# A planner that keeps VectorE and GpSimd apart at a shared port, with its priorities set anew, in a fused attention and two-expert-layer kernel

## The chip, the cores and the metric

The kernel runs on one core of a Trainium2 chip: TensorE (PE) with its weight loads (PEld), VectorE (DVE), ScalarE (ACT), GpSimd (POOL) and the queue engine SyncE (SP). The metric is the device time of one execution in microseconds. Before the change the median of three runs was 1277.99 us (1277.92 to 1278.14).

## The reference

Three steps follow each other on 2304 tokens of 512 numbers. The weights of the dense layer come as 64-bit floats; all else is fp32.

```python
# attention: 4 batches, 8 heads, 576 rows of 64; only the 32 largest scores of a row stay
scores = scale * np.matmul(q, k.transpose(0, 1, 3, 2))
kth = np.partition(scores, -32, axis=-1)[..., -32:-31]
scores = np.where(scores >= kth, scores, -1e9)
attn = softmax(scores);  x = attn @ v            # then heads side by side: (2304, 512)
# dense layer, 512 -> 2048 -> 512
h = x @ w_in;  x = (h * np.cos(h)) @ w_out
# 8 experts, 512 -> 1024 -> 512, one for each token
logits = x @ w_gate;  e_idx = np.argmax(logits, axis=1)
out[mask] = gate_w[mask, None] * eom[mask, e, None] * (np.maximum(x[mask] @ w1[e], 0) @ w2[e])
```

## The kernel before

The program is written as a list of operations (`plan.op`), each with its engine, an assumed length in ns, the buffers that it reads and writes, and a priority number. `Plan.run` plays this list through once while the program is being built, with the assumed lengths: whenever an engine is free it takes, among the operations that can start within 1 ns, the one with the lowest priority number, or else the one that can start first. What comes out is one fixed order for each engine. On the chip each engine works its order off in sequence and waits at semaphores for data and buffers; the assumed times themselves are not in the program. An operation held up on an engine therefore holds up all that stands behind it there.

Attention is cut into 80 units: 64 of two heads by 128 rows ("m") and 16 of two heads by the 64 rows that are left ("x"). In a unit (`attention`) PE transposes the queries (L555) and multiplies with the keys (L573); ACT copies the upper half of the scores (L581); DVE takes maxima and minima of the halves (L587) and finds the 32 largest by MAX8 and MATCH_REPLACE8 (L600, L605, L610); POOL prepares the threshold (L614), ACT and POOL mask the scores (L624, L628), ACT takes the exponential (L631), PE transposes (L652) and multiplies with the values (L683, L686), DVE normalises (L696), ACT and POOL split the result into two parts of less precision (L710, L712). Unit u has priority 10 u, plus an offset for each step from the table `ADD`. `load_heads` (L495 to L522) loads a pair of heads, `LOAD_AHEAD` before its first unit.

Beside it the 64-bit weights of the dense layer are converted in 32 pieces (`narrow`, L721 to L737): a load of 512 KB, two TENSOR_SCALAR on DVE (L722, L724), three ACT operations, an addition and a multiplication on POOL (L733, L735), and a SCALAR_TENSOR_TENSOR on DVE (L737). 16 pieces stay on the core (L745, L747), 16 are split (L755, L757) and stored to memory as `wod`. `CONV_RATE` says how many pieces there are for each unit.

The dense layer works on nine chunks of 256 tokens, eight units each (`moe_unit`, `moe_tail`): 24 matmuls into the hidden layer (L773 to L775), a cosine on ACT (L789), a product on DVE (L812), a split on ACT and POOL (L823, L825), a load of `wod` (L820) and 12 matmuls back (L833 to L835). `MOE_STEP` is the distance in priority from one unit of a chunk to the next. After each chunk `route` finds every token's expert with some 25 small DVE operations (L883 to L925), and POOL scatters the tokens' numbers into a table in memory (L929). The last scatter, reading the table back (L998) and gathering the tokens (L1037) lie between the dense layer and the experts.

The experts' weights are loaded in eight pieces each (L1014), copied by ACT in reduced precision (L1015), and what the copy loses is subtracted out by POOL (L1018) and DVE (L1022) in turn. `turn` transposes an expert's tokens on PE (L1053), with a copy on ACT (L1058) and a subtraction on DVE (L1060); `TURN_AT` sets its place among the matmuls of the expert before (L1077 to L1079, L1095 to L1097).

## Time and profile before

| | |
|---|---|
| median of three runs | 1277.99 us |
| profiled execution | 1275.37 us |
| its span, first to last instruction | 1273.6 us |
| PE busy | 1126.0 us, 88% |
| DVE busy | 881.9 us, 69% |
| ACT busy | 850.7 us, 67% |
| POOL busy | 717.9 us, 56% |

The profile is of one execution. A busy share over the whole span mixes stages: weight conversion beside the first attention units, attention beside the dense layer, and the experts alone. So the rows below are taken by stretches. "Idle before" of an instruction says what its engine waited for.

### The profile page before, as it was taken

How to read it: one execution, taken by the hardware profiler on the slowest of the kernel's cores; microseconds unless marked ns; L12 is line 12 of the kernel's file. 1: busy time of each engine (PE TensorE's matmuls, PEld its weight loads, DVE VectorE, ACT ScalarE, POOL GpSimd, SP SyncE). 2: the span in 40 equal slices, each digit the busy share in tenths (PEclk: the TensorE clock that was granted, in tenths of full speed). 3: DMA queues.
4: the chain of work that ended last, by engine and by line, in shares of the span. 5: the costliest groups of instructions: out<-in, count | busy, mean ns of one | idle time of the engine just before them, and what ended most of it. 6: DMA issues, size and time to landing. Idle time of an engine off the chain costs nothing.

```text
span 1273.6 us, 22562 instructions
## 1 busy us (share of the span) xinstructions
PE 1126.0 (88%) x7524; PEld 931.1 (73%) x7525; DVE 881.9 (69%) x2732; ACT 850.7 (67%) x1852; POOL 717.9 (56%) x1102
## 2 busy tenths in 40 slices
PE   3667778799999999899998989999973999999995
PEld 2444666578787787786776777878962899999994
DVE  6999989896899797979845899886233344443310
ACT  5888797877788887887766688888553344444320
POOL 7898879876546646544643546545447355554400
PEclk9777899989999999999999999999995999999998
DMA  7433325555604444225244403325686244344100
GB/s 196 131 132 126 98 67 173 187 167 186 212 17 130 117 147 133 67 84 166 95 130 130 150 2 109 100 75 164 207 307 212 87 168 158 132 150 156 62 19 25
DMA packets 95806, 164.71 MB, mean 129 GB/s; under 512 B 49850, under 2 KB 54202, under 8 KB 95680
## 3 DMA queue, kind: packets, MB, share of 16 engines
q1 hardware_dynamic: 91264, 153.71, 37.7%
q0 software_dynamic: 4416, 9.47, 2.3%
q8 instruction: 61, 1.00, 0.3%
q14 instruction: 65, 0.53, 0.1%
HBM read 146.72 MB, written 19.56 MB: 131 GB/s over the span
## 4 chain that ended last, share of the span: by engine, by line
PE 43%; DVE 23%; ACT 13%; issue 9%; POOL 8%; DMA 3%; POOLq 0%; SPq 0%; ACTq 0%; DVEq 0%
DVE area_a L600 7%; DVE area_a L605 6%; PE bank L833 3%; DVE area_a L587 3%; PE bank L773 3%; PE bank L834 3%; PE bank L835 3%; PE bank L652 3%; PE bank L774 3%; PE bank L775 3%; PE bank L1077 3%; PE bank L1078 2%; ACT area_g L789 2%; PE bank L1079 2%; PE bank L683 2%
## 5 line engine op out<-in xcount | busy, mean ns | idle before, releaser
L600 DVE MAX8 area_a<-area_a 128x8 f32<-128x288 f32 x576 | 243.5, 447 | 1.2
L628 POOL TENSOR_TENSOR area_a<-area_a 128x576 f32<-128x576 f32 x144 | 187.3, 1312 | 28.4 <-ACT area_a L624 27.8
L605 DVE MATCH_REPLACE8 area_a<-area_a 128x288 f32<-128x288 f32 x432 | 188.9, 442 | 0.0
L773 PE MATMUL bank<-area_f,area_w 128*128 128x256 f32 x576 | 176.5, 306 | 0.3 <-ACT area_a L655 0.2
L774 PE MATMUL bank<-area_f,area_w 128*128 128x256 f32 x576 | 162.5, 282 | 0.0
L775 PE MATMUL bank<-area_f,area_w 128*128 128x256 f32 x576 | 162.2, 282 | 0.0
L587 DVE TENSOR_TENSOR area_a<-bank,area_a 128x288 f32<-128x288 f32 x288 | 121.0, 446 | 48.6 <-ACT area_a L581 24.4
L825 POOL TENSOR_TENSOR area_f<-area_g,area_f 128x256 fp32r<-128x256 f32 x144 | 107.2, 760 | 56.1 <-ACT area_f L823 48.4
L652 PE MATMUL bank<-ident,area_a 128*128 128x128 f32 x576 | 96.4, 296 | 42.6 <-ACT area_a L631 31.2
L833 PE MATMUL bank<-area_l,area_f 128*128 128x512 f32 x288 | 126.3, 439 | 2.1 <-ACT area_f L823 1.1
L624 ACT ACTIVATE area_a<-area_a 128x576 bf16<-128x576 f32 x144 | 106.5, 769 | 30.1 <-POOL area_a L614 29.5
L631 ACT ACTIVATE area_a<-area_a 128x576 f32<-128x576 f32 x144 | 111.4, 774 | 15.7 <-POOL area_a L628 13.8
L652 PEld LDWEIGHTS bank<-ident,area_a 128*128 128x128 f32 x576 | 69.0, 150 | 65.8 <-ACT area_a L631 47.0
L835 PE MATMUL bank<-area_l,area_f 128*128 128x512 f32 x288 | 115.6, 401 | 0.3 <-POOL area_f L825 0.2
L773 PEld LDWEIGHTS bank<-area_f,area_w 128*128 128x128 f32 x576 | 110.5, 192 | 6.8 <-issue 3.1
L834 PE MATMUL bank<-area_l,area_f 128*128 128x512 f32 x288 | 115.1, 400 | 0.0
L573 PE MATMUL bank<-area_a 64*128 64x288 f32 x512 | 96.2, 474 | 18.9 <-ACT area_a L560 15.3
L774 PEld LDWEIGHTS bank<-area_f,area_w 128*128 128x128 f32 x576 | 111.2, 193 | 1.0
L775 PEld LDWEIGHTS bank<-area_f,area_w 128*128 128x128 f32 x576 | 110.2, 191 | 0.0
L655 ACT ACTIVATE area_a<-bank 128x512 f32<-128x512 f32 x144 | 84.8, 596 | 15.9 <-PE bank L652 14.5
L1082 ACT ACTIVATE area_f<-bank 128x384 fp32r<-128x384 f32 x64 | 31.4, 490 | 84.9 <-PE bank L1079 84.9
L683 PE MATMUL bank<-area_a 128*64 128x128 f32 (+1 forms) x1280 | 85.0, 278 | 3.3 <-ACT area_a L668 1.8
(211 smaller groups left out, 2939.7 us busy)
## 6 DMA issues: line engine op xcount, KB each, us to landing
area_l<-wod SPq DMA_DIRECT2D x144, 512.0 KB, 3.9
area_l<-in_moe_w_dram SPq DMA_DIRECT2D x47, 512.0 KB, 4.2
area_n<-in_moe_w_dram SPq DMA_DIRECT2D x17, 512.0 KB, 4.4
area_l<-in_moe_w_in_dram SPq DMA_DIRECT2D x16, 512.0 KB, 4.1
area_l<-in_moe_w_out_dram SPq DMA_DIRECT2D x16, 512.0 KB, 4.1
wod<-area_l SPq DMA_DIRECT2D x16, 512.0 KB, 2.7
area_a<-in_k_dram SPq DMA_DIRECT2D x32, 128.0 KB, 3.0
area_a<-in_q_dram SPq DMA_DIRECT2D x32, 128.0 KB, 3.0
```

Of the source, the lines that this page charges most:

```text
L587: plan.op({"DVE": vec(HALF)}, lambda j=j, to=to, op=op: nc.vector.tensor_tensor(to(), low[j].ap[:, 0:HALF], sc.ap[:, j, HALF:S], op=op), [ ...
L600: lambda j=j, t=t: nc.vector.max(mx.ap[:, j, 8 * t:8 * t + 8], up.ap[:, j, :]),
L605: lambda j=j, t=t: nc.vector.match_replace(up.ap[:, j, :], mx.ap[:, j, 8 * t:8 * t + 8], up.ap[:, j, :], LOWEST),
L628: plan.op({"POOL": 1234.0}, lambda j=j: nc.gpsimd.tensor_tensor(sc.ap[:, j, :], sc.ap[:, j, :], bl.ap[:, j, :], op=OP.subtract), [(bl, j)] ...
L631: plan.op({"ACT": act(S, 2)}, lambda j=j: nc.scalar.activation(sc.ap[:, j, :], sc.ap[:, j, :], AF.Exp, scale=scale, bias=sm.ap[:, j:j + 1] ...
L652: nc.tensor.transpose(pp.ap[:, r_ * P:(r_ + 1) * P], flat[:, at + r_ * P:at + (r_ + 1) * P], ident)
L773: nc.tensor.matmul(o, w_in_h[:, c_, fs], xh[:, c_, :], start=(c_ == 0), stop=False)
L774: nc.tensor.matmul(o, w_in_h[:, c_, fs], xl[:, c_, :], start=False, stop=False)
L775: nc.tensor.matmul(o, w_in_l[:, c_, fs], xh[:, c_, :], start=False, stop=(c_ == KC - 1))
L833: nc.tensor.matmul(acc[t].ap, gh, wr(0), start=(f == 0), stop=False)
L834: nc.tensor.matmul(acc[t].ap, gh, wr(1), start=False, stop=False)
L835: nc.tensor.matmul(acc[t].ap, gl, wr(0), start=False, stop=(f == NF - 1))
```

## The change

Every operation gets a mark `port`. By default it is set for operations of POOL; it is set by hand for VectorE operations that need the second SBUF port (conversion, the cosine product, the routing's small operations, expert weight subtractions), and cleared for POOL's indirect DMAs. In `Plan.run` a marked operation starts no earlier than the end of the last marked operation on the other of the two engines. The constants are set anew: offsets in `ADD`, rates, steps, and a few assumed lengths.

```diff
-ADD = {'q': -10.1,
+ADD = {'q': -8.59,
...
- 's': -13.9,
+       's': -10.77,
...
- 'sub': 4.1,
+       'sub': 21.52,
...
-CONV_RATE = 1.3
+CONV_RATE = 1.25
-TURN_AT = 24.0
+TURN_AT = 25.3
-MOE_STEP = 10.09
-LOAD_AHEAD = 30.8
+MOE_STEP = 12.92
+LOAD_AHEAD = 15.34
...
+        o.port = "POOL" in o.eng if port is None else port
...
+        held = {"DVE": 0.0, "POOL": 0.0}
...
                     late = max(t, free[e])
+                    if o.port:
+                        late = max(late, held["POOL" if e == "DVE" else "DVE"])
...
             free[e] = t + dur
+            if o.port:
+                held[e] = t + dur
...
-            mant(I32), raw()[:, :, 1], 0xFFFFF, None, op0=OP.bitwise_and), [buf], [mb], prio)
+            mant(I32), raw()[:, :, 1], 0xFFFFF, None, op0=OP.bitwise_and), [buf], [mb], prio, port=True)
...
-        plan.op({"DVE": 700.0}, lambda: nc.vector.tensor_tensor(rr.ap, hs.ap, rr.ap, op=OP.mult),
-                [hs], [rr], prio)
+        plan.op({"DVE": 605.0}, lambda: nc.vector.tensor_tensor(rr.ap, hs.ap, rr.ap, op=OP.mult),
+                [hs], [rr], prio, port=True)
...
-            plan.op({"DVE": 90.0}, fn, K(*r) + list(er), K(*w) + list(ew), prio)
+            plan.op({"DVE": 90.0}, fn, K(*r) + list(er), K(*w) + list(ew), prio, port=True)
...
-            plan.op({"POOL": 1100.0}, put, [at, rec, (B_table, "init")], [(B_table, (c, t))], prio, lat=3000.0)
+            plan.op({"POOL": 1300.0}, put, [at, rec, (B_table, "init")], [(B_table, (c, t))], prio, lat=4000.0, port=False)
```

The new lines push everything behind them down: from `load_heads` on, a line of before stands seven lines further down (L722 is L729, L1022 is L1029).

Three places show what becomes of the order. The first is DVE in one of the first attention units, beside the conversion; area_l is the loaded weight piece, area_g, area_h and area_n its parts, area_a holds attention's buffers. Before:

```order
L737 SCALAR_TENSOR_TENSOR area_n<-area_l_278,area_n 128x512
L587 TENSOR_TENSOR area_a<-bank_125,area_a 128x288
L600 MAX area_a<-area_a 128x8
L722 TENSOR_SCALAR area_g<-area_l_357 128x512
L724 TENSOR_SCALAR area_h<-area_l_357 128x512
L592 MAX area_a<-area_a 128x8
L696 TENSOR_TENSOR area_a<-bank_122,area_a 128x128
L722 TENSOR_SCALAR area_g<-area_l_369 128x512
L724 TENSOR_SCALAR area_h<-area_l_369 128x512
L600 MAX area_a<-area_a 128x8
L605 MATCH_REPLACE area_a<-area_a 128x288
L722 TENSOR_SCALAR area_g<-area_l_390 128x512
```

and now, where one unit's maxima are nearly found:

```order
L607 MAX area_a<-area_a 128x8 x2
L612 MATCH_REPLACE area_a<-area_a 128x288 x2
L744 SCALAR_TENSOR_TENSOR area_n<-area_l_297,area_n 128x512
L729 TENSOR_SCALAR area_g<-area_l_366 128x512
L731 TENSOR_SCALAR area_h<-area_l_366 128x512
L729 TENSOR_SCALAR area_g<-area_l_381 128x512
L731 TENSOR_SCALAR area_h<-area_l_381 128x512
L607 MAX area_a<-area_a 128x8 x2
L617 MAX area_a<-area_a 128x8
L594 TENSOR_TENSOR area_a<-bank_126,area_a 128x288
L617 MAX area_a<-area_a 128x8
L594 TENSOR_TENSOR area_a<-bank_126,area_a 128x288
```

The conversion's operations stood singly and in pairs between the maxima; now those of several pieces stand together, five in a row here, between two rounds of the maxima.

The second place is POOL from the last dense-layer splits (L825, now L832) to the first gather: area_a and area_w are the weights of experts 0 and 1, `table` the table of tokens. Before:

```order
L825 TENSOR_TENSOR area_f<-area_g,area_f 128x256 x8
L1018 TENSOR_TENSOR area_a<-area_n,area_a 128x1024
L1018 TENSOR_TENSOR area_a<-area_l_10101,area_a 128x1024
L1018 TENSOR_TENSOR area_w<-area_l_10123,area_w 128x1024
L1018 TENSOR_TENSOR area_w<-area_l_10146,area_w 128x1024
L928 MEMSET spacer 1x1
L929 DMA table<-small 18432x2
L928 MEMSET spacer 1x1
L929 DMA table<-small 18432x2
L1018 TENSOR_TENSOR area_w<-area_l_10159,area_w 128x1024
L1018 TENSOR_TENSOR area_w<-area_n,area_w 128x1024
L1036 MEMSET spacer 1x1
```

and now:

```order
L832 TENSOR_TENSOR area_f<-area_g,area_f 128x256 x7
L1025 TENSOR_TENSOR area_a<-area_n,area_a 128x1024
L1025 TENSOR_TENSOR area_w<-area_l_10105,area_w 128x1024
L1025 TENSOR_TENSOR area_w<-area_n,area_w 128x1024
L1025 TENSOR_TENSOR area_w<-area_l_10152,area_w 128x1024
L1025 TENSOR_TENSOR area_w<-area_l_10162,area_w 128x1024
L935 MEMSET spacer 1x1
L936 DMA table<-small 18432x2
L935 MEMSET spacer 1x1
L936 DMA table<-small 18432x2
L1043 MEMSET spacer 1x1
```

Before, four subtractions stood between the last split and the last two scatters, and two behind the scatters; now five stand ahead of the scatters and none between these and the gather, which begins with the last row.

The third is the start of SP's queue: weight pieces (area_l) and the first two pairs of heads. Before:

```order
L721 DMA area_l_135<-in_moe_w_in_dram 128x1024
L495 DMA area_a<-in_k_dram 128x4x64 x2
L502 DMA area_a<-in_k_dram 64x2x64
L495 DMA area_a<-in_q_dram 128x4x64 x2
L502 DMA area_a<-in_q_dram 64x2x64
L510 DMA area_a<-in_v_dram 128x2x256
L513 DMA area_a<-in_v_dram 64x2x64
L522 DMA area_a<-in_v_dram 64x64
L721 DMA area_l_171<-in_moe_w_in_dram 128x1024
```

and now:

```order
L728 DMA area_l_134<-in_moe_w_in_dram 128x1024
L728 DMA area_l_149<-in_moe_w_in_dram 128x1024
L728 DMA area_l_152<-in_moe_w_in_dram 128x1024
L502 DMA area_a<-in_k_dram 128x4x64 x2
L509 DMA area_a<-in_k_dram 64x2x64
L502 DMA area_a<-in_q_dram 128x4x64 x2
L509 DMA area_a<-in_q_dram 64x2x64
L517 DMA area_a<-in_v_dram 128x2x256
L520 DMA area_a<-in_v_dram 64x2x64
L529 DMA area_a<-in_v_dram 64x64
L728 DMA area_l_184<-in_moe_w_in_dram 128x1024
```

Three weight pieces stand ahead of the first keys, where one stood.

## Rows read from the trace of the kernel before

**Rows 1.** The page's first part: the span; busy time, share and instructions by engine.
```profile
span 1273.6 us, 22562 instructions
...
PE 1126.0 (88%) x7524; PEld 931.1 (73%) x7525; DVE 881.9 (69%) x2732; ACT 850.7 (67%) x1852; POOL 717.9 (56%) x1102
```

**Rows 2.** Busy time by stretches (windows): stretch, length, each engine, clock, DMA.
```profile
12.00:50.00 38.00, 16.24 (x84) 10.95 (x84) 37.48 (x97) 28.00 (x61) 29.64 (x29) 0.92 0.65 170
50.00:200.00 150.00, 111.47 (x715) 83.59 (x715) 144.27 (x437) 127.62 (x283) 129.42 (x162) 0.84 0.35 113
200.00:300.00 100.00, 88.44 (x685) 70.22 (x686) 84.38 (x256) 83.66 (x196) 80.78 (x125) 0.91 0.49 160
300.00:885.00 585.00, 557.57 (x4178) 451.45 (x4177) 482.61 (x1750) 455.62 (x1069) 305.51 (x577) 0.98 0.37 117
885.00:946.00 61.00, 60.00 (x377) 53.25 (x376) 18.77 (x44) 31.66 (x58) 24.50 (x29) 1.00 0.70 231
946.00:981.00 35.00, 8.92 (x51) 6.66 (x49) 15.78 (x35) 16.04 (x21) 24.75 (x24) 0.59 0.79 267
981.00:1260.00 279.00, 278.96 (x1428) 252.73 (x1428) 95.75 (x110) 102.01 (x156) 111.52 (x103) 0.99 0.32 109
```

**Rows 3.** Three lines by source: count, shortest/median/longest in ns, first and last start.
```profile
L722 DVE TENSOR_SCALAR area_g<-area_l x32: 402/516/1360, 5.0 to 283.2; 128x512 int32<-128x512 int32 x32
...
L724 DVE TENSOR_SCALAR area_h<-area_l x32: 402/480/1512, 5.3 to 283.6; 128x512 int32<-128x512 int32 x32
...
L737 DVE SCALAR_TENSOR_TENSOR area_n<-area_l,area_n x32: 664/716/1750, 10.3 to 289.8; 128x512 int32<-128x512 int32 x32
```

**Rows 4.** The same lines by form: busy us, mean ns, idle before.
```profile
L737 DVE SCALAR_TENSOR_TENSOR area_n<-area_l,area_n 128x512 int32<-128x512 int32 x32 | 29.2, 913 | 7.2 <-POOL area_n L735 7.1
...
L724 DVE TENSOR_SCALAR area_h<-area_l 128x512 int32<-128x512 int32 x32 | 25.9, 809 | 0.0
...
L722 DVE TENSOR_SCALAR area_g<-area_l 128x512 int32<-128x512 int32 x32 | 21.7, 678 | 3.1 <-POOL area_f L825 1.3 <-DMA area_l<-in_moe_w_out_dram 1.1 <-DMA area_l<-in_moe_w_in_dram 0.7
```

**Rows 5.** Timeline of POOL and DVE, from 14.5 us: start, length, engine, line.
```profile
14.53 1.27 POOL L733 TENSOR_TENSOR area_n<-area_n,area_g 128x512 f32<-128x512 f32 x1 [1.49 <-ACT area_g L732]
14.72 1.36 DVE L722 TENSOR_SCALAR area_g<-area_l 128x512 int32<-128x512 int32 x1
...
15.88 1.33 POOL L735 TENSOR_TENSOR area_n<-area_n,area_h 128x512 f32<-128x512 f32 x1
...
16.01 1.48 DVE L724 TENSOR_SCALAR area_h<-area_l 128x512 int32<-128x512 int32 x1
```

**Rows 6.** Timeline at the start: the queue engine's loads, the first score operation.
```profile
7.32 1.06 SPq L721 DMA_DIRECT2D area_l<-in_moe_w_in_dram  x2
...
12.02 1.39 DVE L587 TENSOR_TENSOR area_a<-bank,area_a 128x288 f32<-128x288 f32 x3 [0.99 <-ACT area_a L581]
```

**Rows 7.** Timeline of the passage from the dense layer to the experts.
```profile
950.84 7.10 SPq L1014 DMA_DIRECT2D area_l<-in_moe_w_dram  x4
...
959.54 2.70 POOL L1018 TENSOR_TENSOR area_w<-area_l,area_w 128x1024 fp32r<-128x1024 f32 x1 [1.99 <-ACT area_w L1015]
...
959.95 2.32 DVE L909 TENSOR_SCALAR area_t<-area_t 128x2 f32<-128x2 f32 x1
...
962.97 1.73 POOL L929 DMA_INDIRECT table<-small  x1 [0.66 <-DVE small L921]
...
965.00 0.97 POOL L929 DMA_INDIRECT table<-small  x1 [0.21 <-issue]
```

**Rows 8.** Timeline of the first turn inside an expert and its reader.
```profile
1014.50 0.69 DVE L1060 TENSOR_TENSOR area_f<-bank,area_f 128x512 fp32r<-128x512 f32 x1 [0.98 <-ACT area_f L1058]
...
1018.48 0.34 PE L1077 MATMUL bank<-area_f,area_w 128*128 128x384 f32 x1
```

**Rows 9.** DVE by lines from 300 to 885 us: the operation that waits for scores.
```profile
L587 DVE TENSOR_TENSOR area_a<-bank,area_a 128x288 f32<-128x288 f32 x200 | 84.1, 446 | 43.1 <-ACT area_a L581 20.7 <-ACT area_a L595 12.2 <-PE bank L573 9.3
```

More of the change, by code (lines that the diff above doesn't have):

```diff
@@ L31 @@
 PATIENCE = {"PE": 1.0, "ACT": 1.0, "DVE": 1.0, "POOL": 1.0, "SP": 1.0}
-ADD = {'q': -10.1,
- 'low': 4.0,
- 's': -13.9,
- 'top': 4.5,
- 'mask': 4.2,
- 'sub': 4.1,
- 'exp': 4.0,
- 'sum': -2.9,
- 'pt': 5.6,
- 'av': 6.0,
- 'norm': -2.2,
- 'xh': 6.0,
- 'conv': 0.0,
- 'tail': 5.0}
-CONV_RATE = 1.3
+ADD = {'q': -8.59,
+       'low': 2.38,
+       's': -10.77,
+       'top': 9.31,
+       'mask': 4.2,
+       'sub': 21.52,
+       'exp': 4.0,
+       'sum': -3.07,
+       'pt': 4.74,
+       'av': 6.15,
+       'norm': -8.85,
+       'xh': 18.42,
+       'conv': -4.55,
+       'tail': 11.44}
+CONV_RATE = 1.25
 CONV_MIX = 2
@@ L85 @@
     __slots__ = ("eng", "fn", "bufs", "deps", "users", "wait", "prio", "lat", "ready", "end", "seq", "done",
-                 "kind")
+                 "kind", "port")
 class Plan:
@@ L116, in fixed, with op @@
         return b
-    def op(self, eng, fn, r=(), w=(), prio=0.0, lat=0.0, kind=None, hold=()):
+    def op(self, eng, fn, r=(), w=(), prio=0.0, lat=0.0, kind=None, hold=(), port=None):
         o = Op()
@@ L722, in narrow @@
         plan.op({"DVE": 335.0}, lambda: nc.vector.tensor_scalar(
-            mant(I32), raw()[:, :, 1], 0xFFFFF, None, op0=OP.bitwise_and), [buf], [mb], prio)
+            mant(I32), raw()[:, :, 1], 0xFFFFF, None, op0=OP.bitwise_and), [buf], [mb], prio, port=True)
         plan.op({"DVE": 335.0}, lambda: nc.vector.tensor_scalar(
             expo(I32), raw()[:, :, 1], 20, 0x7FF, op0=OP.logical_shift_right, op1=OP.bitwise_and),
-            [buf], [eb], prio)
+            [buf], [eb], prio, port=True)
         plan.op({"ACT": 613.0}, lambda: nc.scalar.activation(
@@ L738, in narrow @@
             fr.ap.bitcast(I32), raw()[:, :, 1], -2 ** 31, fr.ap.bitcast(I32), op0=OP.bitwise_and,
-            op1=OP.bitwise_or), [buf], [fr], prio)
+            op1=OP.bitwise_or), [buf], [fr], prio, port=True)
         return fr, buf
@@ L1023, in load_expert @@
                     hl(1), raw.ap, hl(0).bitcast(F32), op=OP.subtract),
-                    [raw, (to, (part, 0))], [(to, (part, 1))], prio + i)
+                    [raw, (to, (part, 0))], [(to, (part, 1))], prio + i, port=True)
         return n1, n2
@@ L1040, in get @@
                     bounds_check=NT - 1, oob_is_err=False)
-            plan.op({"POOL": 1200.0}, get, [tb, B_x2d], [(xg, t)], prio, lat=2500.0)
+            plan.op({"POOL": 1300.0}, get, [tb, B_x2d], [(xg, t)], prio, lat=2500.0, port=False)
         return xg
@@ L1114, in put @@
                 puts.append(st)
-            plan.op({"POOL": 1200.0}, put, [y, tb], [(B_out, (e, t))], prio + 30, lat=3000.0)
+            plan.op({"POOL": 1300.0}, put, [y, tb], [(B_out, (e, t))], prio + 30, lat=3000.0, port=False)
     held = [load_expert(0)]
```

## The prediction, made before the changed kernel ran

> **What bounds the kernel now.** I read the page's first part, then a table of stretches, then the lines of the VectorE operations that the change marks, then single moments. The span is 1273.6 us and PE is busy for 1126.0 of it, DVE for 881.9 [rows 1]; these are averages over stages with different limits, so the table of stretches decides [rows 2]. From 12 to 50 us and from 50 to 200 us DVE is busy 37.48 of 38.00 and 144.27 of 150.00 us, while PE has 16.24 and 111.47: DVE sets the pace there. From 200 to 300 us nothing is full (PE 88.44, DVE 84.38, POOL 80.78 of 100). From 300 to 885 us PE has 557.57 of 585.00 and DVE 482.61: PE sets the pace, with 27.4 us of its own idle time. From 885 us, when the last attention unit's products end, to 946 us PE is at 60.00 of 61.00. From 946 to 981 us everything waits (PE 8.92 of 35): that is the passage from the dense layer to the experts. From 981 to 1260 us PE is at 278.96 of 279.00, and no order of the other engines can shorten that.
>
> So an edit can reach the end by three ways only: DVE time before 200 us, PE's idle time until 946 us, and the 35 us of the passage.
>
> **The change part by part.**
>
> *The operations that are kept apart.* In the weight conversion each of 32 pieces has two TENSOR_SCALAR and one SCALAR_TENSOR_TENSOR on DVE (L722, L724, L737). Their shortest executions are 402, 402 and 664 ns [rows 3]; their means are 678, 809 and 913 ns [rows 4]. The excess is 32 x 0.276 = 8.8, 32 x 0.407 = 13.0 and 32 x 0.249 = 8.0 us, in all 29.8 us over 96 operations, 0.31 us each. What it consists of is seen at 14.7 us: POOL runs an addition from 14.53 for 1.27 us, and L722, started at 14.72, lasts 1.36 us, until just behind it; POOL's next addition runs from 15.88, and L724, started at 16.01, lasts 1.48 us [rows 5]. So a wait costs about 1.0 us (0.96 and 1.08 over the shortest), and the medians of 516, 480 and 716 ns [rows 3] say that more than half of the 96 hardly wait: some 30 of them carry the whole sum.
> The Trainium skill, SBUF — State Buffer, section Who interferes with whom, says that VectorE and GpSimd share one pair of SBUF ports as an exclusive lock held for a whole instruction, and that issue order decides who blocks. The two moments above agree with it. By that rule a planner that only orders instructions keeps the two apart only as far as its clock is the chip's; what this would give stands as the second rival.
> In the new order the 96 operations stand in 29 unbroken runs on DVE where they stood in 71 (counted in the order). If only the first of a run meets a POOL operation under way, 29.8 x 29/71 = 12.2 us of waiting are left and 17.6 are saved. The ends are nothing saved, or all 29.8; and below nothing, since within a run POOL can take a turn between any two, as at 14.7 us. I take 17.6 because the moments show waiting only where POOL has work queued, and a run is put where POOL waits for DVE's row maxima. Of this only what falls where DVE sets the pace counts: the pieces start between 5 and 290 us [rows 3], evenly enough, and 188 of the 288 us from 12 to 300 are such [rows 2]; 17.6 x 188/288 = 11.5 us. Later DVE has cover: PE is the later one. The other marked operations (L812, the routing's small ones) lie behind 200 us, under PE: nothing.
>
> *The start.* Three conversion loads of 512 KB stand before the first head's loads on SP where one stood. Two such issues took 1.06 us [rows 6], so the first scores come at least that much later; if the two transfers (1.05 MB) have to pass first, at the 170 GB/s of 12 to 50 us [rows 2], 6.2 us. In exchange DVE, which has its first score operation at 12.02 us [rows 6], does three pairs of conversion operations meanwhile, 6 x 0.402 = 2.4 us that it would do later. Net -1.3 to +3.8; I take +1.0, near the issue time.
>
> *The dense layer is spread wider and attention's second half later.* At the last attention unit PE has in its order 10.0 first-product and 14.2 second-product units of the dense layer left, where it had 8.1 and 12.0 (counted in the order; a unit is 24 or 12 matmuls). The 20.1 units of before took PE's 60.0 us from 885 to 946 [rows 2], 2.99 us each; 4.1 more are 12.2 us moved behind the attention. PE, which has them no longer to do before, was 95.3% busy there, so the stretch before shortens by about as much; the idle 4.7% are lost: +0.6. Ends: nothing, or the whole 12.2 if attention were held by something else.
>
> *The passage.* Before, GpSimd's last two table scatters stood behind four weight subtractions of experts 0 and 1; now behind five, the last of them on the eighth expert load behind the last dense-layer load, where it was the seventh. On DVE three subtractions stand between the routing operations, where one stood. All of these wait for loads, and on an in-order engine the routing waits with them. Four such loads were issued within 7.10 us [rows 7], 2.4 us from one to the next: +2.4. Against it, the first scatter took 1.73 us beside a DVE subtraction and the second 0.97 [rows 7]; in the new order all of expert 1's subtractions are over by then: -0.8. The wait of L909, 2.32 us behind POOL's subtraction of 2.70 us [rows 7], may recur or not: the ends are -3 and +6. I take +1.6.
>
> *The experts.* The transposes of the next expert's tokens stand nine matmuls later. Before, the last DVE operation of such a turn ended at 1014.50 + 0.69 = 1015.19 us and its first reader on PE started at 1018.48 [rows 8]: 3.29 us of cover. Eight experts have 576 matmuls of 512 columns and 768 of 384, half of the columns each; 279 us [rows 2] / 2 / 576 = 0.24 us for one of 512, nine are 2.2 us. Cover of 1.1 us is left: 0; if it were gone, each 1 us is seven times on the path. The changed lengths and latencies of the planner's DMA entries only move the order.
>
> *Sum.* -11.5 + 1.0 + 0.6 + 1.6 = -8.3 us. The profiled execution took 1275.37 us, its span plus 1.8 around it; it lies 2.6 under the median of 1277.99. With -8.3 it gives 1267.1, and the median 1269.7 us.
>
> **Rivals.**
> 1. *Better overlap than counted.* In the new order the scores stand about one unit further ahead of the rest of attention. DVE's idle time before L587, which waits for scores and their copies, is 43.1 us from 300 to 885 us [rows 9], and PE's own 27.4 [rows 2]. If half of PE's goes, -13.7 more: 1256.0 us. For it: all those waits are of attention's first steps, which now stand earlier. Against it: DVE's idle time there is no loss while PE is later, and PE's order has as many dependences as before.
> 2. *It does not do what it says.* No wait or semaphore keeps the two engines apart; only the order changes. If after some tens of us chip and plan have drifted apart, collisions are as frequent as before: the 29.8 us stay, the small terms cancel, and the time stays at 1278 us. For it: the present order knew nothing of the port and yet lets two thirds of the operations through, so this may be as good as chance gets. Against it: POOL's and DVE's streams wait for each other in every unit, which pulls them back into step.
> 3. *The runs collide (slower).* In a run of four to six marked operations POOL, if it has work queued, takes a turn after each, as at 14.7 us, where each lost about 1.0 us. If half of the 96 wait so: 96/2 x 1.02 = 48.9, less 29.8, is 19.1 us more, x 188/288 = 12.4 us in the stretch that counts; with the +3.2 of start, overlap and passage 1293.6 us. It decides from 0.31 us of mean wait upward. For it: POOL is busy 129.42 of 150 us from 50 to 200 us [rows 2], so a long run finds it free only if it waits for DVE itself. Against it: that is where the runs stand, and of POOL's next conversion operation the inputs come out of the run.
>
> **How the numbers follow.** Forecast 0.42 (1262 to 1275 for this case alone), first rival 0.18, second 0.16, third 0.24. A change under 0.2% (2.6 us) is taken as none, since a measurement can't tell it apart. Faster: 0.42 + 0.18 = 0.60; same 0.16; slower 0.24. The range goes from 1250, beyond the first rival's 1256 by half of PE's remaining 13.7 us, to 1288, which takes in the weaker half of the third (a mean wait up to 0.42 us): about 0.07 are left below and 0.10 above.
>
> **What would show it.** Means of the three conversion lines (now L729, L731, L744) towards 0.55, 0.57 and 0.77 us if the runs work, unchanged for the second rival, above 0.7, 0.85 and 0.95 for the third. The stretch in which DVE is full should end some 10 us earlier, the last attention product some 20 us earlier than 885 us (8 from the sum, 12 from the work moved behind it), and PE's dense tail be 72 us long. From the last dense matmul to the first expert matmul 35 to 38 us. The expert stage 279 us as before; if PE idles there before its first matmul of an expert, the cover of the turn was misjudged. The prediction is wrong if the conversion lines shorten and the last attention product doesn't come earlier (then DVE did not set the pace), or if they stay and the time still falls.

## The result, and the profile after

The changed kernel takes 1243.12 us (median of 4 runs, 1242.16 to 1244.57) against 1278.07 beside it, ratio 0.9727, interval 0.9710 to 0.9744. The forecast was 1269.7 us with a range from 1250: the direction was right, but the time fell by 35 us instead of 8. The two profiled executions lie 31.8 us of span apart, since the one before took 2.7 us less than its median; all stages below are of these two.

First the page of the changed kernel: span, and busy time by engine.

```profile
span 1241.8 us, 22569 instructions
...
PE 1107.6 (89%) x7524; PEld 924.3 (74%) x7525; DVE 850.0 (68%) x2732; ACT 843.2 (68%) x1852; POOL 714.5 (58%) x1102
```

The work is the same, yet PE is busy for 18.4 us less than in [rows 1] and DVE for 31.9. Which stage gave the time is read from windows cut at the kernel's own events: the end of the 24th attention unit (its last product, L686/L689 of before, L693/L696 now), called unit 24 below, the end of the 80th, the last dense matmul, the first expert matmul. The first table is the kernel before, cut so (stretch, length, busy time and count of PE, PEld, DVE, ACT, POOL, granted clock, DMA share, GB/s); the second is the changed kernel.

```profile
12.00:298.30 286.30, 214.73 (x1473) 163.58 (x1474) 265.68 (x786) 237.58 (x535) 238.14 (x311) 0.87 0.44 136
298.30:885.10 586.80, 559.09 (x4188) 452.73 (x4189) 483.06 (x1752) 457.32 (x1072) 307.21 (x581) 0.98 0.38 118
885.10:946.40 61.30, 60.30 (x377) 53.15 (x375) 18.77 (x44) 32.05 (x59) 24.50 (x29) 1.00 0.70 233
```

```profile
12.00:303.60 291.60, 225.71 (x1533) 172.91 (x1533) 262.25 (x811) 240.50 (x550) 240.52 (x321) 0.84 0.47 150
303.60:841.10 537.50, 521.33 (x4063) 427.46 (x4064) 461.82 (x1724) 442.86 (x1054) 303.21 (x567) 1.00 0.36 114
841.10:916.00 74.90, 71.95 (x448) 63.20 (x447) 18.22 (x46) 36.94 (x65) 32.14 (x33) 1.00 0.72 248
916.00:950.00 34.00, 8.32 (x49) 6.43 (x48) 12.99 (x34) 12.94 (x17) 18.25 (x21) 0.57 0.64 219
950.00:1228.50 278.50, 278.46 (x1428) 253.18 (x1428) 88.35 (x110) 102.80 (x156) 107.19 (x103) 0.99 0.33 110
```

The start did not get shorter: unit 24 ends at 303.6 us instead of 298.3. The passage has 34.0 us where the same cuts of before give 34.4, the experts 278.5 where they gave 279.5. The whole gain lies between unit 24 and the last dense matmul, the stretch that PE sets: 586.8 + 61.3 = 648.1 us before, 537.5 + 74.9 = 612.4 now, **35.7 us less**.

What PE lost there before is seen in two sums. Its idle time over the two stretches falls from 28.7 to 19.1 us. Its busy time falls by 26.1: some 6.3 of that are 2.1 dense units that the new order puts ahead of unit 24 (counted in the order, at the prediction's 2.99 us each), 1.2 are one more unit's scores ahead of it, and about 19 are matmuls that take less time. For at most 10 of these the granted clock answers; what shortened the rest no run here shows. These are four windows of the kernel before:

```profile
645.00:660.00 15.00, 13.28 (x107) 11.94 (x106) 6.88 (x34) 11.93 (x28) 4.13 (x10) 0.95 0.41 117
660.00:675.00 15.00, 15.00 (x98) 10.81 (x98) 10.17 (x32) 7.92 (x23) 9.30 (x22) 0.94 0.62 187
690.00:705.00 15.00, 10.53 (x76) 8.10 (x73) 8.55 (x24) 11.74 (x25) 6.09 (x12) 0.81 0.14 47
705.00:720.00 15.00, 15.00 (x107) 10.89 (x106) 12.78 (x45) 9.17 (x27) 8.11 (x18) 0.96 0.62 211
```

From 690 to 705 us PE has work for 10.53 of 15 us, the clock (full 2.4 GHz, low 1.2 GHz) averages 0.81 of full, and in the window behind it PE is busy throughout and still has 0.96: here a gap cost its own length and came with slower matmuls after it. Of 39 such windows from 300 to 885 us seven were below 0.99; their shortfall adds to 10.05 us of full clock, which is what it cost at most, since PE was idle for a part of it. In the changed kernel none of 36 windows from 300 to 840 us is below.

The waits name the gaps that are seen. The longest ones of PE in the stretch, before (waiting line, what it waited for, total us, times, longest):

```profile
PE bank L652 <- ACT area_a L631: 5.9, 7, 3.9
PE bank L652 <- ACT area_a L581: 3.5, 2, 3.3
PE bank L686 <- ACT area_a L668: 2.7, 1, 2.7
```

And after:

```profile
PE bank L580 <- ACT area_a L567: 5.7, 12, 1.3
...
PE bank L659 <- ACT area_a L638: 0.5, 1, 0.5
```

The transposes of the probabilities (L652, now L659) hardly wait for the exponential (L631, now L638) any more. By the order, scores are now 2.94 units ahead of the products (mean from unit 24 to 76), where they were 1.60 ahead.

Last, the conversion lines by form (busy us, mean ns, idle before), which answer to [rows 4]:

```profile
L744 DVE SCALAR_TENSOR_TENSOR area_n<-area_l,area_n 128x512 int32<-128x512 int32 x32 | 27.3, 870 | 5.2 <-POOL area_n L742 5.2
...
L729 DVE TENSOR_SCALAR area_g<-area_l 128x512 int32<-128x512 int32 x32 | 22.0, 689 | 4.4 <-DMA area_l<-in_moe_w_in_dram 2.7 <-POOL area_f L832 1.7
...
L731 DVE TENSOR_SCALAR area_h<-area_l 128x512 int32<-128x512 int32 x32 | 19.2, 602 | 0.0
```

Their excess over the shortest executions of before (402, 402, 664 ns) is 22.2 us. It was 29.8; forecast were 12.2.

### The profile page after: what moved, and what is told of

It is laid out like the page before. It is cut to its first block, busy times and chain, and to the rows that moved or that the text cites. A ratio compares the mean times of both kernels' runs of the same rounds, so it can differ in the third digit from the quotient of the medians.

```text
span 1241.8 us, 22569 instructions
## 1 busy us (share of the span) xinstructions
PE 1107.6 (89%) x7524; PEld 924.3 (74%) x7525; DVE 850.0 (68%) x2732; ACT 843.2 (68%) x1852; POOL 714.5 (58%) x1102
## 4 chain that ended last, share of the span: by engine, by line
PE 42%; DVE 25%; ACT 14%; issue 9%; POOL 6%; DMA 2%; SPq 0%; POOLq 0%; ACTq 0%; DVEq 0%
DVE area_a L607 7%; DVE area_a L612 7%; DVE area_a L594 4%; PE bank L690 3%; PE bank L840 3%; PE bank L780 3%; PE bank L580 3%; PE bank L1085 3%; PE bank L1084 3%; PE bank L841 3%; PE bank L842 3%; PE bank L1086 3%; PE bank L782 2%; PE bank L781 2%; PE bank L1104 2%
## 5 line engine op out<-in xcount | busy, mean ns | idle before, releaser
L635 POOL TENSOR_TENSOR area_a<-area_a 128x576 f32<-128x576 f32 x144 | 184.8, 1293 | 27.8 <-ACT area_a L631 27.1
L780 PE MATMUL bank<-area_f,area_w 128*128 128x256 f32 x576 | 169.0, 293 | 2.5 <-ACT area_h L786 1.8
L781 PE MATMUL bank<-area_f,area_w 128*128 128x256 f32 x576 | 162.1, 281 | 0.0
L782 PE MATMUL bank<-area_f,area_w 128*128 128x256 f32 x576 | 162.0, 281 | 0.0
L832 POOL TENSOR_TENSOR area_f<-area_g,area_f 128x256 fp32r<-128x256 f32 x144 | 109.2, 770 | 66.1 <-ACT area_f L830 63.0
L631 ACT ACTIVATE area_a<-area_a 128x576 bf16<-128x576 f32 x144 | 107.3, 778 | 38.5 <-POOL area_a L621 35.1
L840 PE MATMUL bank<-area_l,area_f 128*128 128x512 f32 x288 | 122.7, 426 | 3.0 <-DMA area_l<-wod 2.9
L638 ACT ACTIVATE area_a<-area_a 128x576 f32<-128x576 f32 x144 | 112.7, 783 | 13.2 <-POOL area_a L635 12.7
L780 PEld LDWEIGHTS bank<-area_f,area_w 128*128 128x128 f32 x576 | 110.0, 191 | 6.4 <-ACT area_h L786 2.1
L842 PE MATMUL bank<-area_l,area_f 128*128 128x512 f32 x288 | 113.8, 395 | 0.5 <-POOL area_f L832 0.5
L841 PE MATMUL bank<-area_l,area_f 128*128 128x512 f32 x288 | 113.4, 394 | 0.0
L580 PE MATMUL bank<-area_a 64*128 64x288 f32 x512 | 94.9, 478 | 12.5 <-ACT area_a L567 11.6
L659 PE MATMUL bank<-ident,area_a 128*128 128x128 f32 x576 | 85.8, 285 | 22.7 <-ACT area_a L638 18.0
L659 PEld LDWEIGHTS bank<-ident,area_a 128*128 128x128 f32 x576 | 67.0, 146 | 37.3 <-ACT area_a L638 21.8
L690 PEld LDWEIGHTS bank<-area_a 128*64 128x64 f32 x1280 | 69.0, 145 | 30.2 <-issue 7.8
L690 PE MATMUL bank<-area_a 128*64 128x128 f32 (+1 forms) x1280 | 87.9, 282 | 1.8 <-ACT area_a L662 0.8
```

The costliest lines, as they stand in the source:

```text
L635: plan.op({"POOL": 1234.0}, lambda j=j: nc.gpsimd.tensor_tensor(sc.ap[:, j, :], sc.ap[:, j, :], bl.ap[:, j, :], op=OP.subtract), [(bl, j)] ...
L659: nc.tensor.transpose(pp.ap[:, r_ * P:(r_ + 1) * P], flat[:, at + r_ * P:at + (r_ + 1) * P], ident)
L690: nc.tensor.matmul(o.ap[j * D:(j + 1) * D, 0:w], vr.ap[:, j, r_, :], rh, start=(r_ == 0), stop=False)
L780: nc.tensor.matmul(o, w_in_h[:, c_, fs], xh[:, c_, :], start=(c_ == 0), stop=False)
L781: nc.tensor.matmul(o, w_in_h[:, c_, fs], xl[:, c_, :], start=False, stop=False)
L782: nc.tensor.matmul(o, w_in_l[:, c_, fs], xh[:, c_, :], start=False, stop=(c_ == KC - 1))
```

## Experiments

The theories, by the letters that the expectations use. A: the lead of the scores (`ADD['sub']`) relieves PE. B: the port rule makes the gain. C: the wider spread of the dense layer (`MOE_STEP`) makes it. D: no constant alone, a joint fit or the luck of one order. E: the spread with the dense tail's offset (`ADD['tail']`). F: the offsets of attention's first steps. G: the late split (`xh`). H: a set of at least spread, tail and lead. I: the lead gains behind unit 24 and costs before it, and the constants that place the conversion give the start back.

All stage times below are each kernel's own profile, cut as above. One profile is one execution, and executions of one kernel lay up to 9 us apart; the column "profiled" has the time of the one whose stages are given, and a few us carry a claim only where several kernels agree. How much dense work is done by unit 24 differs with the order: the column "units" counts it (first and second products, of 144), and the adjusted column is the stretch from unit 24 to the last dense matmul with the work put back, plus 2.99 us for each unit over before's 22.5. It counts dense work only. By the cut 144 score matmuls have ended in e14, 152 in e15 and in the changed kernel, 136 in e5; eight are a unit's, and take PE 1.2 us (median of 64 in the kernel before), so a longer lead moves one or two such units as well.

| kernel | median us | profiled | unit 24 ends | units | 24 to last dense matmul | adjusted | passage | conversion excess |
|---|---|---|---|---|---|---|---|---|
| before | 1278.07 | 1275.37 | 298.3 | 22.5 | 648.1 | 648.1 | 34.4 | 29.8 |
| after | 1243.12 | 1243.50 | 303.6 | 24.6 | 612.4 | 618.7 | 34.0 | 22.2 |
| e1 constants, no port rule | 1265.35 | 1265.75 | 309.3 | 23.5 | 628.1 | 631.1 | 33.7 | 30.4 |
| e2 port rule, old constants | 1264.10 | 1263.49 | 294.7 | 22.4 | 638.4 | 638.1 | 37.5 | 7.7 |
| e3 after, old offsets | 1268.72 | 1264.74 | 297.8 | 23.1 | 638.1 | 639.9 | 35.7 | 16.6 |
| e4 after, old rates | 1255.17 | 1251.06 | 317.1 | 27.8 | 605.6 | 621.4 | 35.0 | 22.0 |
| e5 after, old sub | 1249.39 | 1252.91 | 297.4 | 22.9 | 628.5 | 629.7 | 33.7 | 15.8 |
| e6 e2, new sub | 1278.26 | 1273.06 | 314.3 | 28.5 | 627.8 | 645.7 | 37.0 | 13.3 |
| e7 after, old MOE_STEP | 1260.34 | 1258.76 | 285.0 | 19.0 | 645.0 | 634.5 | 35.3 | 17.4 |
| e8 after, nudged | 1246.45 | 1246.75 | 297.5 | 22.2 | 620.9 | 620.0 | 34.6 | 22.8 |
| e9 after, old tail | 1253.24 | 1250.14 | 301.7 | 25.1 | 618.9 | 626.7 | 35.4 | 17.6 |
| e10 after, old first steps | 1249.96 | 1249.36 | 302.1 | 24.5 | 618.6 | 624.6 | 34.8 | 14.8 |
| e11 after, old xh | 1238.91 | 1239.30 | 291.3 | 22.7 | 619.8 | 620.4 | 34.4 | 19.2 |
| e12 before, nudged | 1279.40 | 1278.70 | 293.0 | 21.5 | 656.0 | 653.0 | 35.4 | 27.6 |
| e13 e2, new MOE_STEP | 1273.40 | 1275.04 | 297.9 | 22.0 | 647.8 | 646.3 | 35.9 | 9.2 |
| e14 e13, new tail | 1262.12 | 1263.64 | 295.8 | 22.2 | 639.5 | 638.6 | 34.2 | 13.4 |
| e15 e14, new sub | 1253.03 | 1253.57 | 306.6 | 23.5 | 618.9 | 621.9 | 35.2 | 23.3 |
| e16 e15, new first steps | 1254.02 | 1257.95 | 313.5 | 23.5 | 616.0 | 619.0 | 34.7 | 11.6 |
| e17 e16, new norm | 1253.82 | 1253.90 | 308.7 | 23.5 | 616.0 | 619.0 | 35.3 | 13.9 |
| e18 e16, new conversion | 1237.77 | 1234.45 | 289.2 | 22.7 | 618.7 | 619.3 | 34.0 | 18.9 |

### The two halves of the change (e1, e2)

e1 leaves the new constants and takes the rule away; e2 has the rule, its marks and lengths, and every constant of before.

```diff
# e1
-                    if o.port:
-                        late = max(late, held["POOL" if e == "DVE" else "DVE"])
# e2: ADD, CONV_RATE, TURN_AT, MOE_STEP, LOAD_AHEAD as before
```

> The changed kernel without the port rule in the planner (marks, lengths and all constants stay). Its order has 66 conversion runs on DVE (29 with the rule), scores 2.90 units ahead of attention's last products (2.94), the same dense backlog. Theory A (the gain is the lead of the scores in the stretch where PE sets the pace; the port rule gives little): 1243 to 1255 us, attention from unit 24 to 80 still near 540 us, clock 1.00 there, conversion operations back to about 30 us of excess. Theory B (the port rule makes the gain): 1265 us or more.

> The changed kernel with all constants of before (offsets, rates, steps), the port rule and the new assumed lengths kept. 40 conversion runs, scores 1.62 units ahead (1.60 before), backlog as before. Theory A: 1268 to 1280 us, units 24 to 80 still near 585 us with the clock at 0.98. Theory B: 1245 to 1255 us.

e1: 0.9891 (0.9864 to 0.9919). e2: 0.9890 (0.9870 to 0.9910). e1 is in B's range and above A's, e2 in neither: neither theory holds alone. Each half alone is worth 12 to 14 us, together they give 35: with the new constants the rule is worth 21 to 22 us (e1 against after), and with the rule the constants are worth 21 (e2 against after). What the rule alone does to the collisions is plain from e2's conversion lines:

```profile
L744 DVE SCALAR_TENSOR_TENSOR area_n<-area_l,area_n 128x512 int32<-128x512 int32 x32 | 22.3, 713 | 7.6 <-POOL area_n L742 7.6
L731 DVE TENSOR_SCALAR area_h<-area_l 128x512 int32<-128x512 int32 x32 | 16.3, 510 | 1.6 <-DMA area_l<-in_moe_w_in_dram 1.6
L729 DVE TENSOR_SCALAR area_g<-area_l 128x512 int32<-128x512 int32 x32 | 15.6, 486 | 1.1 <-DMA area_l<-in_moe_w_in_dram 0.9 <-POOL area_f L832 0.2
```

The excess is 7.7 us there. But e2's windows to unit 24 and behind it show what became of the saving:

```profile
12.00:294.70 282.70, 212.23 (x1470) 162.23 (x1470) 244.25 (x785) 235.22 (x533) 239.83 (x310) 0.86 0.44 138
294.70:874.50 579.80, 557.45 (x4205) 454.08 (x4206) 476.83 (x1757) 459.20 (x1082) 301.65 (x582) 0.99 0.38 120
874.50:933.10 58.60, 57.63 (x362) 50.55 (x362) 18.37 (x41) 27.44 (x53) 25.36 (x29) 1.00 0.70 236
```

DVE is busy 21.4 us less before unit 24 (265.68 to 244.25), its idle time there grows from 20.6 to 38.5, and unit 24 ends only 3.6 us earlier. The largest of its new waits is for attention's products, 9.6 us in e2 (first row); the same pair of lines (L696, L686) stood at 2.6 us before (second).

```profile
DVE area_a L703 <- PE bank L693: 9.6, 10, 3.4
```

```profile
DVE area_a L696 <- PE bank L686: 2.6, 3, 1.8
```

So of what the rule saved DVE, five sixths were gone by unit 24, and most of e2's gain lies behind it, 9.7 us; how the rule gives PE that time is not shown, and its size, from two profiles, is not far above their scatter (e12 below has 656.0 us there where before has 648.1).

### Which constants: halves and single ones (e3 to e7, e9 to e11)

```diff
# e3: ADD of before, all else new
# e4: CONV_RATE 1.3, TURN_AT 24.0, MOE_STEP 10.09, LOAD_AHEAD 30.8, ADD new
# e5 (on after)
-       'sub': 21.52,
+       'sub': 4.1,
# e6 (on e2)
-       'sub': 4.1,
+       'sub': 21.52,
```

> The changed kernel with the table ADD of before alone; port rule, rates and steps stay new. Scores 1.56 units ahead, dense backlog 10.0 and 13.5 units as in the changed kernel, 34 conversion runs. Theory A: most of the gain is gone, 1262 to 1278 us. Theory C (the wider spread of the dense layer, MOE_STEP, makes the gain): 1243 to 1252 us. Theory B: 1243 to 1255 us.

> The changed kernel with CONV_RATE, TURN_AT, MOE_STEP and LOAD_AHEAD of before; port rule and offsets stay new. Scores 2.94 units ahead, backlog 8.0 and 11.5 units as before. Theory A: 1240 to 1252 us. Theory C: 1262 us or more. Experts' stage unchanged at 279 us whatever the turn's place.

> The changed kernel with one number of before: the offset of the mask subtraction, 'sub', 4.1 for 21.52 (all that follows it in a unit inherits at least this). Scores 1.67 units ahead of attention's last products (2.94), dense backlog 10.0 and 14.2 units as in the changed kernel, 32 conversion runs. Theory A (the lead is what relieves PE from unit 24 to 80): that stretch goes from 537 to 560 us or more, the time to 1260 to 1272 us, PE's wait of L659 for ACT's exponential comes back. Theory D (no single constant, only the joint fit or luck): 1243 to 1255 us.

> All constants of before but 'sub' 21.52, with the port rule. Lead 2.92, backlog 8.0 and 11.0 units as before, 38 conversion runs. Theory A: 1248 to 1257 us, as with all new offsets and old rates (1255.2), units 24 to 80 near 545 us. Theory D: 1260 to 1268 us, near the port rule alone (1264.1).

e3 0.9928 (0.9907 to 0.9948), e4 0.9824 (0.9800 to 0.9847), e5 0.9767 (0.9749 to 0.9786), e6 0.9999 (0.9982 to 1.0016). By the adjusted column the offsets (e4: 621.4 us) do more for PE's stretch than the rates (e3: 639.9). Against the changed kernel e4's profile loses 13.5 us up to unit 24, of which 3.2 dense units are 9.6, and 2.7 behind it (adjusted); that execution took 4.1 us less than e4's median. e3 came out in A's range, e4 in neither A's nor C's, e5 in D's, e6 in neither A's nor D's. By the end time theory A fell: the lead is worth 6 us in the new table and costs 14 in the old. By stages the new one gains 11.0 us behind unit 24, 629.7 (e5) to 618.7 (after), adjusted, of which two units of scores are 2.3, against 6.2 at the start, of which 1.7 more dense units are up to 5.1; e5's profile took 3.5 us more than its median, so the 11.0 are rather too many. In the old one it gains PE nothing (638.1 to 645.7). There 6.1 more dense units stand ahead of unit 24, which ends 19.6 us later, and PE's waits behind it have moved and grown: its idle time over the two stretches is 34.6 us, where e2 has 23.3. These are e6's largest:

```profile
PE bank L670 <- ACT area_a L588: 11.3, 4, 2.9
PE bank L780 <- ACT area_a L567: 7.9, 4, 2.7
...
PE bank L659 <- DVE area_a L707: 0.4, 1, 0.4
```

The transposes (L659) no longer wait, but the transposes of the probabilities' last columns (L670) wait behind the scores' copies (L588), and dense matmuls (L780) behind ACT's copy of the queries (L567). So a lead was worth something to PE only with a dense layer that is placed to go with it.

```diff
# on after, one kernel each
-MOE_STEP = 12.92            # e7
+MOE_STEP = 10.09
-       'tail': 11.44}       # e9
+       'tail': 5.0}
# e10: q, low, s, top, sum, pt, av of ADD as before
-       'xh': 18.42,         # e11
+       'xh': 6.0,
```

> The changed kernel with MOE_STEP 10.09 alone. Lead 2.94, backlog 8.0 and 11.5 units. If the wider spread of the dense layer is what lies between old rates (1255.2) and the changed kernel (1243.1): 1252 to 1258 us, with the first 24 units ending near 317 us as there. If it was another rate: 1241 to 1248 us.

> The new kernel with the 'tail' offset alone at 5.0, as it was. Theory E (the dense layer's second products must be held back as far as the new offset holds them, or they crowd PE while attention's chain waits): most of what the offsets gave beside MOE_STEP goes, 1254 to 1264 us, and PE's stretch from unit 24 to 80 is 550 us or longer. Theory F (it is the order of attention's first steps, q, s, top, that must fit MOE_STEP): 1243 to 1248 us. Theory D (no constant alone carries it): 1246 to 1253 us.

> The new kernel with the offsets of attention's first steps and of its row sums and products (q, low, s, top, sum, pt, av) as they were; sub, norm, xh, tail and all rates new. Theory F: 1254 to 1266 us, since these place the scores against the dense layer. Theory E: 1243 to 1248 us. Theory D: 1246 to 1253 us.

> The new kernel with the 'xh' offset alone (the split of a unit's output on VectorE, GpSimd and ScalarE for the dense layer) at 6.0, as it was. Theories E and F both: 1243 to 1248 us. If the late split is what frees VectorE and GpSimd for the next unit's maxima (theory G): 1252 to 1262 us. Theory D: 1246 to 1253 us.

e7 0.9862 (0.9845 to 0.9878), e9 0.9813 (0.9775 to 0.9851), e10 0.9780 (0.9757 to 0.9803), e11 0.9690 (0.9665 to 0.9716). Taking the new value out singly loses 17 us for `MOE_STEP`, 10 for `tail`, 7 for the first steps, and gains 4 for `xh`. e9 and e10 lie in or just above D's range, e7 is 2 us above what was expected, and the 4 us of `xh` are within what a permuted order can move (next section). No single one carries the gain; theories F and G fall, C and E are bounded.

### How far an order scatters (e8, e12)

```diff
# e8 (on after): q -8.69, s -10.87, top 9.41, sub 21.62, av 6.05, xh 18.32, tail 11.54
-MOE_STEP = 12.92
+MOE_STEP = 12.85
# e12 (on before): q -10.0, s -13.8, top 4.6, sub 4.2, av 5.9, xh 5.9, tail 5.1
```

> The changed kernel with seven offsets moved by 0.1 to 0.2 and MOE_STEP 12.85: lead 2.94, backlog 10.0 and 14.2, 32 runs, all as in the changed kernel, but another order in detail. Theory A: 1243 us within some 6 us, which is then the scatter of one order against another of the same shape. Theory D: 1255 us or more, the fit being luck of one order.

> The kernel before with seven of its offsets moved by 0.1, a hundredth of a unit: the same number of conversion runs, scores as far ahead, nearly the same work behind the last unit. It measures how far the time of one and the same plan scatters with the order's small permutations. If the fit is real and the old table was an ordinary one: 1273 to 1283 us, in which case a difference between two orders of under 5 us says little of a constant. If orders scatter widely (part of the gain is the luck of a draw): beyond 1268 or 1288 us.

e8 0.9750 (0.9731 to 0.9770), e12 1.0008 (0.9996 to 1.0020). A nudge that only permutes neighbours moved the time by 1 to 3 us, once for each table. So the gain is no lucky draw, and differences under some 5 us between two of these kernels say little of a constant.

### Building the table up from the port rule (e13 to e18)

```diff
# e13 = e2 and
+MOE_STEP = 12.92
# e14 = e13 and
+       'tail': 11.44
# e15 = e14 and
+       'sub': 21.52
# e16 = e15 and the new q, low, s, top, sum, pt, av
# e17 = e16 and
+       'norm': -8.85
# e18 = e16 and
+       'conv': -4.55; CONV_RATE = 1.25; TURN_AT = 25.3; LOAD_AHEAD = 15.34
```

> The table of before with the port rule and MOE_STEP alone at 12.92. Theory C (the wider spread alone, 17 us as taken out of the finished table): 1245 to 1252 us. Theory E (it needs the new 'tail') and theory H (a set of at least three: step, tail and lead): 1260 to 1270 us, near the port rule's 1264.

> As the run with the port rule and MOE_STEP 12.92, with 'tail' at 11.44 too. Theory E: 1245 to 1253 us. Theory H: 1256 to 1268 us. Theory C: 1245 to 1252 us, no change from the run without 'tail'.

> With 'sub' at 21.52 too, so that the scores stand three units ahead. Theory H (the lead pays only where the dense layer is spread and its second products are held back): 1242 to 1252 us, against 1278 us for the same lead on the old MOE_STEP and 'tail'. Theory E: within 5 us of the run without 'sub'. If the lead costs here too (over 1264 us), the first steps' offsets are what is missing.

> With the offsets of the first steps (q, low, s, top, sum, pt, av) new as well; norm, xh, conv, CONV_RATE, TURN_AT and LOAD_AHEAD stay as they were. If these six carry nothing: 1237 to 1247 us, the changed kernel's time or, by 'xh', a little below. If the whole table is one fit: 1250 to 1262 us.

e13 0.9969 (0.9954 to 0.9985): the spread alone makes the port rule's kernel 9 us slower, which none of the theories had. e14 0.9872 (0.9840 to 0.9903): the tail's offset takes that back, as theory H had it and E and C had not. e15 0.9802 (0.9778 to 0.9825), 1 us above H's range: now the lead pays 9 us, and by stages, e14 against e15, 638.6 to 621.9 us behind unit 24 (adjusted; one unit of scores is 1.2 of these 16.7), against 10.8 us at unit 24, of which the 1.3 more dense units are at most 3.9. PE's longest waits of the transposes in the stretch, e14 first:

```profile
PE bank L659 <- ACT area_a L638: 8.2, 10, 3.7
PE bank L659 <- ACT area_a L588: 4.7, 3, 3.4
```

```profile
PE bank L659 <- ACT area_a L588: 1.5, 2, 0.9
PE bank L659 <- ACT area_a L638: 1.0, 3, 0.4
```

12.9 us of waits of the transposes become 2.5, in two kernels that differ in `sub` alone. But this is not where the 16.7 us are, since other waits grow:

```profile
PE bank L580 <- ACT area_a L567: 6.4, 8, 1.9
PE bank L670 <- ACT area_a L588: 4.2, 1, 4.2
```

The first of these was 3.1 us in e14. The two stretches in both, e14 first:

```profile
295.80:864.70 568.90, 548.91 (x4145) 445.01 (x4146) 473.31 (x1759) 457.31 (x1078) 306.86 (x582) 0.98 0.36 114
864.70:935.30 70.60, 68.06 (x419) 59.53 (x417) 20.51 (x46) 35.74 (x63) 31.27 (x32) 1.00 0.77 254
```

```profile
306.60:851.30 544.70, 525.94 (x4086) 432.45 (x4085) 467.67 (x1750) 448.05 (x1062) 305.84 (x574) 0.99 0.36 112
851.30:925.50 74.20, 72.27 (x449) 63.15 (x447) 18.13 (x46) 36.95 (x65) 32.12 (x33) 1.00 0.75 250
```

PE's idle time falls by 1.8 us only, from 22.5 to 20.7, and its busy time by 18.8, of which the moved dense units and scores are 5.1. The shortfall of the granted clock, 10.2 us of full clock in e14 and 3.4 in e15, answers for at most 6.8; the other 7 are open. From e5 to the changed kernel, too, the idle time stays (19.9 and 19.1). That the lead makes the gain is shown by these pairs; that it does so by PE's visible waits is not.

e16 0.9803 (0.9778 to 0.9829): the first steps add nothing to the end time; theory H's set is short by 10 us. The stage times show where they are: behind unit 24, e16 is as good as after (619.0 and 618.7, adjusted), but its unit 24 ends at 313.5 us, in a profile that took 3.9 us more than e16's median.

> The table built up so far (MOE_STEP, 'tail', 'sub' and the first steps' offsets new on the port rule) with 'norm' at -8.85 too. If the lead's cost lies at the start, in DVE and GpSimd having the scores' copies before the conversion (theory I), 'norm' can't mend it: 1249 to 1258 us and unit 24 ends at 308 us or later. If the early release of the products' bank counts: 1239 to 1248 us with the stretch behind unit 24 shorter than 612 us.

> The same table with 'norm' as before and 'conv' -4.55, CONV_RATE 1.25, LOAD_AHEAD 15.34 and TURN_AT 25.3 instead. Theory I: the conversion placed earlier gives the start back, unit 24 ends at 290 to 304 us, the stretch behind it stays 612 to 622 us, and the time is 1237 to 1247 us. If it is 'norm': 1249 to 1258 us.

e17 0.9810 (0.9783 to 0.9837), e18 0.9695 (0.9669 to 0.9722): the four constants `conv`, `CONV_RATE`, `TURN_AT` and `LOAD_AHEAD`, and not `norm`. The windows of e16 and then e18:

```profile
12.00:313.50 301.50, 224.28 (x1509) 173.08 (x1509) 248.65 (x799) 238.88 (x544) 237.44 (x320) 0.85 0.46 146
313.50:854.80 541.30, 523.37 (x4081) 431.55 (x4080) 461.88 (x1738) 445.55 (x1061) 304.30 (x570) 1.00 0.36 113
```

```profile
12.00:289.20 277.20, 214.73 (x1499) 162.51 (x1499) 252.74 (x791) 235.78 (x537) 233.98 (x314) 0.85 0.47 149
289.20:834.90 545.70, 528.31 (x4099) 433.35 (x4098) 466.18 (x1743) 447.82 (x1068) 306.74 (x575) 1.00 0.38 117
```

DVE has about the same work to unit 24 (248.65 and 252.74) and is idle for 52.9 us in e16, for 24.5 in e18. Its two longest waits there, e16 and e18:

```profile
DVE area_a L703 <- PE bank L693: 15.6, 11, 2.9
DVE area_a L594 <- ACT area_a L588: 9.2, 5, 2.9
```

```profile
DVE area_a L703 <- PE bank L693: 7.3, 6, 2.3
DVE area_a L594 <- ACT area_a L588: 5.1, 3, 3.7
```

Theory I holds in the main: unit 24 ends 24.3 us earlier, of which 0.8 dense units fewer are 2.4, and the stretch behind it is the same (619.0 and 619.3, adjusted). The 24.3 are too many, since e16's profile is its slowest execution and e18's its fastest; the medians differ by 16. It is not fewer collisions: the conversion's excess is 11.6 us in e16 and 18.9 in e18. Which of the four constants does it (`LOAD_AHEAD` places loads of heads, not the conversion), and what they do without the lead, was not tried.

e18 is also the fastest kernel: 1237.77 us (1234.45 to 1240.06), below the changed kernel's lowest run of 1242.16; the two did not run side by side, and their intervals against before overlap a little (0.9669 to 0.9722, 0.9710 to 0.9744). It differs from it in `norm` and `xh` alone, which stay at the values of before; e11, with `xh` alone put back, has 1238.91.

## Why the prediction was wrong

**The step that failed** is the third, "the dense layer is spread wider and attention's second half later", with +0.6 us. With the start's +1.0 and the passage's +1.6 all the new constants stood at +3.2 together. Measured, they give -11.6 us without the port rule (e1) and -21 with it (e2 against after). The step argued that 12.2 us of dense work moved behind the attention shorten the stretch before by as much and lose only cover. The move came about (tail 74.9 us; 72 foretold), but the step priced moved work alone: it had no term for what a new order of the scores, the products and the dense layer does to PE's own time in that stretch. Built up singly on the port rule the spread costs 9 us (e13), the tail's offset gives 11 (e14), the lead 9 (e15) and the four constants of e18 16.

**The first rival named the cause, gave it 0.18 and too small a size, and had the means only in part.** Its ground, scores about one unit further ahead (by the mean it is 1.3), is what e14 and e15 show: 16.7 us behind unit 24 for the lead alone, some 15 without the moved scores, on a dense layer that is spread to go with it. It allowed half of PE's visible idle time, 13.7 us. Idle time was no ceiling: it fell by 9.6 us and matmul time by 26.1, of which 7.5 are moved work. The prediction's list of three ways to the end has the same gap: it counts PE's idle time until 946 us and not PE's busy time, though the clock stood at 0.98 of full from 300 to 885 us in [rows 2]. The counterargument, that DVE's idle time is no loss while PE is later, looked at the wrong engine's waits; PE's own, L652 behind L631, were in the trace and were not priced.

**The port term, -11.5, came near by luck and was wrong in its steps.** With the old constants the rule measures -12.85 us; with the new ones, for which the term was made, -22 (e1 against after). And its saving on the conversion is 22.1 us in e2 and 7.6 in the changed kernel, while the number of unbroken runs is 40 and 29: fewer runs did not mean fewer collisions, so "excess times 29/71" has no support. And the factor 188/288, all DVE time before 200 us reaching the end, failed too: DVE saved 21.4 us up to unit 24 and the unit came 3.6 earlier, as products on PE were late next (9.6 us of waits, 2.6 before).

**The second rival** (the order can't keep the engines apart on chip) is out as stated: with the rule alone the excess falls from 29.8 to 7.7 us, without it the new constants leave 30.4. In the changed kernel it is half true, at 22.2. The Trainium skill, SBUF — State Buffer, section Who interferes with whom, has issue order decide who blocks. e2 agrees in so far as its instructions are those of before in another order, and 22.1 us of waiting are gone. **The third rival** (runs collide, 1293.6) is out: the means are 0.689, 0.602 and 0.870 us, below the 0.7, 0.85 and 0.95 that it wanted.

**The small terms.** Start: the forecast held that extra conversion loads cost about 1 us; unit 24 is 5.3 us later with 6.3 us more dense work done by then, so this profile can't price it. Passage: +1.6 forecast, -0.4 measured; the scatters, at 1.73 and 0.97 us in [rows 7], are both short now:

```profile
935.70 0.99 POOL L936 DMA_INDIRECT table<-small  x1 [2.87 <-DVE cnt L1156]
...
936.99 0.97 POOL L936 DMA_INDIRECT table<-small  x1 [0.21 <-issue]
```

Experts: 0 forecast, 278.5 for 279.5 us. The cover of the turn, 3.29 us in [rows 8], was put at 1.1 and is 987.16 - (985.22 + 0.69) = 1.25:

```profile
985.22 0.69 DVE L1067 TENSOR_TENSOR area_f<-bank,area_f 128x512 fp32r<-128x512 f32 x1 [0.97 <-ACT area_f L1065]
...
987.16 0.34 PE L1084 MATMUL bank<-area_f,area_w 128*128 128x384 f32 x1
```

**The test that the prediction set itself** gave the sign: the last attention product was to come 20 us earlier than 885 and came 44 earlier, with the conversion lines little shorter. "If they stay and the time still falls", the prediction is wrong: nearly so.

**Still open:** what makes PE's matmuls shorter beyond the clock; why the rule is worth some 9 us more with the new constants than without, though it then removes fewer collisions of the conversion (8.2 us from e1 to after, 22.1 from before to e2; those of the experts' subtractions, L1022 and L1029, which lie where PE is full, fall in both); why the spread alone (e13) costs 9 us; and why the old `MOE_STEP` costs PE's stretch 16 us with the other rates new (e7, 634.5 adjusted) and 3 with them old (e4).

## What to carry to other kernels

Cut the windows at the program's own events and compare experiments stage by stage: one constant took 11 and 17 us out of PE's stretch and cost some 1 and 7 at the start, with the moved dense work counted on both sides, and did no good in another table, which its end times alone (6 us better, 14 worse) did not tell; and count how much work an order has moved across a cut before reading the two sides. A list of waits shows which gap went, not what it was worth: add up the engine's idle and busy time on both sides before a wait is called the cause. PE's idle time was no upper bound for what a better order gave it; its gaps came with slower work around them. Time saved on an engine that is full reaches the end only as far as the next wait lets it: name that wait before counting the saving.
